# A late mask build, DMA transposes for half of a layernorm's blocks, and retuned instruction priorities in a fused attention and mixer layer

## The chip, the cores and the metric

The kernel runs on one core of one Trainium2 chip. The metric is the device time of the core in microseconds (us); a profile of one execution gives a span that is about 2 us shorter. A run counts as slow when it takes over 1.5% more than the fastest of its kernel. Engines: TensorE (PE; PEld is its weight load), VectorE (DVE), ScalarE (ACT), GpSimd (POOL), and SyncE (SP), which issues all DMAs of this kernel from one queue.

## The reference, cut to what matters

```
x [2048, 448] bf16
h   = x + A(layernorm(x))     # A: q,k,v = x@wqkv; 16 heads; each token sees 8 keys
                              #    at distances 0,2,..,14; softmax; @ wo
h2  = h + B(layernorm(h))     # B: z = gelu(x@w_in); z1, z2 = halves; z2 = layernorm(z2)
                              #    g = w_sp[2048,2048] @ z2 + b_sp; (z1*g) @ w_out
```

The token axis is cut into 16 blocks of 128. "LN1" is the first layernorm. QK products are made for groups of four blocks, so there are four QK groups of four TensorE pairs each. "Mixing" is the product with `w_sp`.

## The kernel before: the parts that matter

The program builds a graph of tasks. Each task has engines that may run it, an assumed duration, and a priority. A list scheduler then fixes the order of instructions on every engine when the kernel is built. Nothing is reordered on the chip: an engine runs its list in order and waits on semaphores. SP is such an engine too, and a DMA's assumed duration on it is the price of issuing it.

```
DMA_US = 2.6                                # assumed: from issue to landing
P = dict(ln_s=0.26, ln_o=5.43, qk_s=2.72, ..., npt=4, nlt=15)   # priorities, tuned by search

def dma_t(dst, src, us, ...):               # DMA transpose; callers pass us = 1.3
    return G.add([("sp", us)], [lambda e: e.dma_start(dst(), src(), transpose=True)], ...)

def layernorm(m, i, prio):                  # i = 0: LN1, i = 1: the second layernorm
    ... bn_stats, bn_aggr (DVE); rstd (POOL); normalise into tring[:, slot] (DVE)
    if i:                                   # second layernorm: one DMA transpose, 128x512
        dma_t(lambda: xB[:, m, :, :], lambda: tring[:, t.slot, :], 1.3, [t], [rm], prio)
        ...
        return
    # LN1: four 128x128 transposes on TensorE into PSUM, one copy out
    G.add([("pe", 0.27)], [e.transpose(psb[...], tring[:, t.slot, c*128:(c+1)*128], ident) for c in range(4)], ...)
    G.add([("act", ...), ("dve", ...)], [copy_on(e, xm, psb[...])], ...)     # xm = xT[:, :, 128m:128m+128]
    if m < P["npt"]:                        # swap of partition halves: two copies ...
        ... copy_on(e, um[ps, 0:3, :], xm[po, 0:3, :])
    elif m % 4 == 3:                        # ... or, for four blocks together, two DMAs
        dma(... e.dma_start(xU[dst, :, cols], xT[src, 0:3, cols]) ...)
```

A QK group needs `xT` (transposed LN1) and `xU` (the same with its partition halves swapped) of its four blocks. The ring `tring` has six slots.

The softmax here doesn't subtract the row's maximum and nothing guards it: scores larger than these inputs give would overflow.

## Time and profile before

The median is 261.2 us; the profiled span is 259.2 us.

| stage | us from the start |
|---|---|
| first statistics aggregated (DVE) | 6.80 |
| first QK pair starts | 16.9 |
| second QK group starts | 34.9 |
| third QK group starts | 47.8 |
| mixing starts | 138.2 |
| end | 259.2 |

From the page of the kernel before: busy tenths of TensorE in 40 equal slices of the span, and the TensorE clock granted, in tenths of full speed.

```profile
PE   6788699999999999799999999999999999999995
PEclk9999799999999999999999999999999999999999
```

TensorE is busy nearly everywhere after the fifth slice. In the fifth slice, the second of the two with a dip, the clock drops to 7 tenths, its lowest. The chain of waits (start us, duration us, what) of the kernel before:

```profile
4.39 1.32 DVE z1p L491
6.97 0.52 DVE st L557
...
16.98 6.17 PE psum L613 x56
...
29.70 1.50 PE psum L621 x4
...
34.95 6.15 PE psum L613 x56
...
106.02 3.23 DMA xS<-xB
...
138.20 10.74 PE psum L771 x49
```

L491 is an integer operation of the mask build. It stands behind the first block's statistics (2.88 us), but ahead of their aggregation (6.80 us) and of the statistics of the next blocks (L557). The four value matmuls at 29.70 us take 1.50 us, about twice the usual 0.77: the granted clock there was 0.50. TensorE had idled 3.0 us before, in three gaps of 0.5, 0.6 and 1.9 us. What SP issues between 20 and 60 us (timeline view; start, us, engine, line, operation, count):

```profile
24.77 1.29 SPq L594 DMA_DIRECT2D xU<-wsp  x2
26.11 4.00 SPq L529 DMA_DIRECT2D w<-in_B_w_in_dram  x6
43.18 2.63 SPq L594 DMA_DIRECT2D xU<-wsp  x4
51.69 5.00 SPq L450 DMA_TRANSPOSE xB<-tring  x3
```

And the second layernorm's DMA transposes, as the view of the tile `tring` gives them (duration in ns: min/median/max):

```profile
L450 SPq DMA_TRANSPOSE xB<-tring x16: 1188/1266/2611, 51.7 to 117.2; - x16
```

A 128x512 DMA transpose keeps the SP queue for about 1.27 us, and a half swap, a plain DMA, for about 0.62 us.

### The profile page before, as it was taken

To read this page: it belongs to the slowest core of one execution; us is meant where nothing else is said; L and a number is where in the kernel's file an instruction comes from. 1 tells how busy PE (TensorE), PEld (TensorE's weight loads), DVE (VectorE), ACT (ScalarE), POOL (GpSimd) and SP (SyncE) were. 2 spreads that over 40 slices of the span, in tenths; PEclk is the share of its full clock that TensorE was granted. 3 is DMA by queue.
4 is the path that set the end of the run, shared out by engine and by line. 5 is a ranking of instruction groups with operands and counts; after the bars stand their busy time and mean duration, and the time that the engine had idled before them with its cause. 6 is when DMAs were issued, how large, how long until landed. Compare 5 with 4: busy or idle time off the path is not lost.

```text
span 259.2 us, 5020 instructions
## 1 busy us (share of the span) xinstructions
PE 244.4 (94%) x2065; PEld 122.2 (47%) x2076; DVE 158.2 (61%) x359; ACT 97.0 (37%) x117; POOL 48.1 (19%) x123
## 2 busy tenths in 40 slices
PE   6788699999999999799999999999999999999995
PEld 2334455455556454355454444544444444444442
DVE  4989888977999999869880008433333333333333
ACT  2147768698897988456663000000000000000000
POOL 7444313220030335425350000000000000000000
PEclk9999799999999999999999999999999999999999
DMA  5992701332122545555436414444044440010002
GB/s 148 296 262 71 169 0 30 96 71 54 43 43 65 89 100 110 130 118 107 108 79 184 97 27 101 101 102 114 0 101 101 104 91 0 25 48 0 0 0 71
DMA packets 58102, 22.41 MB, mean 86 GB/s; under 512 B 48096, under 2 KB 56928, under 8 KB 58080
## 3 DMA queue, kind: packets, MB, share of 16 engines
q1 hardware_dynamic: 58080, 22.10, 36.4%
q8 instruction: 16, 0.26, 0.4%
q14 instruction: 6, 0.05, 0.1%
HBM read 6.49 MB, written 1.84 MB: 32 GB/s over the span
## 4 chain that ended last, share of the span: by engine, by line
PE 87%; DVE 5%; ACT 2%; POOL 1%; DMA 1%; issue 1%; SPq 1%; DVEq 0%; POOLq 0%
PE psum L771 37%; PE psum L613 25%; PE psum L621 10%; PE psum L789 8%; PE psum L675 3%; PE psum L654 2%; PE psum L687 2%; ACT z1p L663 1%; DMA xS<-xB 1%; DVE st L557 1%; PE psum L580 1%; SPq L450 1%; DVE xU L599 1%; DVE tring L562 1%; DVE z1p L491 1%
## 5 line engine op out<-in xcount | busy, mean ns | idle before, releaser
L776 DVE TENSOR_TENSOR qk<-psum,bb 128x512 bf16<-128x512 f32 x28 | 19.3, 690 | 68.3 <-PE psum L771 68.3
L771 PE MATMUL psum<-early,z2p 128*128 128x512 bf16 x218 | 48.5, 379 | 0.3
L771 PE MATMUL psum<-wsp,z2p 128*128 128x512 bf16 x219 | 48.4, 379 | 0.4 <-issue 0.2
L663 ACT ACTIVATE z1p<-psum 128x912 bf16<-128x912 f32 (+2 forms) x36 | 33.5, 933 | 3.4 <-PE psum L654 2.9
L771 PEld LDWEIGHTS psum<-wsp,z2p 128*128 128x128 bf16 x224 | 21.9, 98 | 26.5 <-issue 0.4
L771 PEld LDWEIGHTS psum<-early,z2p 128*128 128x128 bf16 x224 | 22.0, 98 | 26.3
L604 POOL TENSOR_TENSOR rstd<-va,mhalf 128x1 f32<-128x1 f32 x48 | 31.4, 656 | 3.8
L602 POOL TENSOR_SCALAR va<-mv 128x1 f32<-128x1 f32 x48 | 11.1, 233 | 81.4 <-DVE mv L559 64.4
L613 PE MATMUL psum<-wsp,early 64*128 64x512 bf16 x128 | 25.0, 376 | 0.0
L613 PE MATMUL psum<-w,xB 64*128 64x448 bf16 x112 | 22.8, 349 | 2.2 <-DMA xS<-xB 1.7
L613 PE MATMUL psum<-xU,early 64*128 64x512 bf16 x96 | 23.3, 377 | 0.0
L613 PE MATMUL psum<-w,xS 64*128 64x448 bf16 x112 | 22.9, 350 | 0.0
L598 ACT ACTIVATE qk<-psum 128x1024 bf16<-128x1024 f32 (+1 forms) x21 | 19.0, 909 | 7.8 <-PE psum L613 7.8
L789 PE MATMUL psum<-xS,z1p 128*128 128x448 bf16 x112 | 21.8, 352 | 0.0
L613 PE MATMUL psum<-xB,w 64*128 64x512 bf16 x98 | 21.8, 376 | 0.0
L613 PE MATMUL psum<-xS,w 64*128 64x512 bf16 x98 | 21.8, 376 | 0.0
L741 DVE BATCH_NORM_STATS2 st<-z2p 128x6 f32<-128x448 bf16 x32 | 19.4, 608 | 3.6 <-ACT z2p L737 3.1
L670 DVE TENSOR_TENSOR z1p<-z1p,maskb 128x1824 bf16<-128x1824 bf16 (+2 forms) x18 | 19.9, 1103 | 1.6 <-ACT z1p L663 1.5
L557 DVE BATCH_NORM_STATS2 st<-x_tm 128x6 f32<-128x448 bf16 x32 | 19.4, 605 | 1.6 <-DMA x_tm<-in_A_x_dram 1.5
L621 PE MATMUL psum<-early,wsp 128*128 128x448 bf16 (+2 forms) x72 | 17.4, 371 | 0.6 <-DVE wsp L599 0.5
L737 ACT ACTIVATE z2p<-psum 128x896 bf16<-128x896 f32 x16 | 14.4, 917 | 8.0 <-PE psum L613 8.0
L763 ACT ACTIVATE z1p<-psum 128x1024 bf16<-128x1024 f32 x14 | 14.3, 1023 | 8.2 <-PE psum L613 8.2
(67 smaller groups left out, 274.5 us busy)
## 6 DMA issues: line engine op xcount, KB each, us to landing
xS<-xB SPq DMA_DIRECT2D x16, 128.0 KB, 2.4
out_dram<-tring SPq DMA_DIRECT2D x16, 112.0 KB, 1.7
xU<-wsp SPq DMA_DIRECT2D x6, 192.0 KB, 3.0
x_tm<-in_A_x_dram SPq DMA_DIRECT2D x1, 896.0 KB, 8.7
w<-in_B_w_in_dram SPq DMA_DIRECT2D x8, 112.0 KB, 3.2
early<-in_A_wqkv_dram SPq DMA_DIRECT2D x2, 392.0 KB, 5.8
w<-in_B_w_in_dram SPq DMA_DIRECT2D x2, 392.0 KB, 7.9
xS<-in_B_w_out_dram SPq DMA_DIRECT2D x1, 784.0 KB, 4.5
```

Source lines behind the costliest of these rows:

```text
L557: G.add([("dve", dve_us(D))], [lambda e: e.bn_stats(st[:, s.slot, 0:6], x_tm[:, m, :])], [r_x[m]], [s], [s], prio=prio)
L598: return e.activation(dst, src, AF.Copy)
L604: G.add([("pool", 0.61)], [lambda e: e.tensor_tensor(rstd[:, k:k + 1], va[:, k:k + 1], mhalf[:, 0:1], ALU.pow)], [r_va[k], r_half], [r_rs[ ...
L613: return [lambda e, j=j, u=u: e.matmul(bank2(b, j, n), ws(j, (LO, HI)[j], u), xs(j, (LO, HI)[j], u), start=(u == 0), stop=(u == 6), tile_p ...
L621: return [lambda e, c=c: e.matmul(bank(b, n, 0, m), ws(ALL, c), xs(ALL, c), start=(c == 0), stop=(c == NCH - 1)) for c in range(NCH)]
L663: lambda e, hh=hh: e.activation(E[0:nk, ev.slot, hh * 4:hh * 4 + 8, 0:nq].rearrange("p (b g) q -> p b g q", b=2), banks(lb, hh, 512, nk).r ...
L670: lambda e: e.tensor_tensor(E[0:nk, ev.slot, :, 0:nq], E[0:nk, ev.slot, :, 0:nq], maskb[0:nk, mi:mi + 1, 0:nq].to_broadcast([nk, NHEAD, nq ...
L737: lambda e, zb=zb, m=m: e.activation(z2p[:, m, :].rearrange("p (b c) -> p b c", b=2), banks(zb, 0, D), AF.Gelu_apprx_tanh)],
L741: lambda e, h=h, m=m, s=s: e.bn_stats(st[:, s.slot, 6 * h:6 * h + 6], z2p[:, m, D * h:D * (h + 1)])],
L771: lambda e, s=s: e.matmul(bank(b, 512), z2p[:, s, fc * 128:(fc + 1) * 128], w[:, s, :], start=(s == 0), stop=(s == NB - 1)) for s in range ...
L776: G.add([("dve", dve_us(512))], [lambda e: e.tensor_tensor(ub[:, u.slot, :], bank(b, 512), bb[:, 512 * tc:512 * (tc + 1)], ALU.add)], [b, ...
L789: lambda e, f=f: e.matmul(bank(b, D), z1p[:, f, 128 * m:128 * m + 128], w_out[:, f, :], start=(f == 0), stop=(f == FC7 - 1)) for f in rang ...
```

## The change

The intent: take the mask build out of the way of the first layernorm; move LN1's transposes of blocks 8 to 15 from TensorE, and their copies from DVE and ScalarE, to the DMA queue; order the last output blocks; and choose the priorities anew for the new graph. Cut to its core:

```diff
+P_TR_US = 0.45
-P = dict(ln_s=0.26, ..., z0=74.82, ..., z1=110.69, ..., npt=4, nlt=15)
+P = dict(ln_s=0.9, ..., z0=150.45, ..., z1=116.86, ..., npt=8, nld=8, mc=25.81)
 ...   # the five mask operations
-            G.add([("dve", 0.2)], [fn], rd, wr, prio=-3.0)
+            G.add([("dve", 0.28)], [fn], rd, wr, prio=P["mc"])
 ...   # layernorm(m, 0, ...)
+            if m < P["nld"]:
                 (TensorE transposes and copy, as before)
+            else:
+                for c in range(NCH):
+                    G.add([("sp", P_TR_US)], [lambda e, c=c: e.dma_start(xm[:, c, :],
+                          tring[:, t.slot, 128 * c:128 * c + 128], transpose=True)],
+                          [t], [], adds=[rm], prio=prio)
 ...   # wout_block
-                    [b] if lo else [], prio=prio, keep=0 if lo else 1)
+                    [b] if lo else [], prio=prio + (m % 4) * 0.1 + (0.05 if lo else 0.0), keep=0 if lo else 1)
```

`npt=8` also moves the half swap of blocks 4 to 7 from DMAs to copies.

## The prediction

> **What bounds it now.** The busy table has TensorE at 94% of a 259.2 us span. By stretches (windows view), from 138 us to the end TensorE runs 28 mixing tiles and 16 output blocks with no gap (117.3 of 121 us); the change cannot shorten that. The time lost lies earlier.
> 1. Start. The chain of waits runs over POOL memsets, then the int32 mask operation (1.31 us on DVE at 4.39 us), then the first layernorm. DVE's statistics of block 0 begin at 2.88 us, but their aggregation runs only at 6.80 us, behind the mask build (2.5 us busy, 0.9 us wait). The first QK pair starts at 16.9 us.
> 2. After the first QK pairs, 24 to 29 us, TensorE idles some 3 us, and its granted clock falls to 0.50 from 30 to 32.5 us (four value matmuls take 1.50 us instead of 0.77). The second QK group starts only at 34.9 us. The Trainium skill ("TensorE: Matmul & The Clock Gate", rules for kernels) says idle of over about 3 us halves the clock; the trace agrees.
> 3. At 107.7 us TensorE waits 1.7 us for the swapped-half DMA of the last blocks.
> In 35 to 104 us TensorE, DVE (90%) and ScalarE (83%) are all nearly full.
>
> **What the change does.**
> - Mask build late: up to 2.5 us of DVE leaves the first layernorm's chain. The QK weights' DMA and their 7 copies (from 13.3 us) limit the gain: first QK pair at about 15 us, gain 1.5 to 2.5 us.
> - Blocks 8 to 15 by DMA: removes 32 transposes from TensorE (4 took 0.25 to 0.4 us) and 8 copies (DVE 0.42, ScalarE 0.60 us): about 2 us TensorE, 3.5 to 4.5 us DVE/ScalarE. Adds 32 DMA transposes on the SP queue. A 128x512 one takes 1.26 us to issue, 2.5 us to land; I estimate 0.3 to 0.6 us issue for a quarter. Latency per block grows from about 1 us to 3 or 4 us, then the half-swap DMA (3 us). SP is nearly idle at 15 to 50 us, so this should hide.
> - Half swap of blocks 4 to 7 by copies, not DMA: adds 8 copies of 0.29 us on DVE (or 0.48 on ScalarE), but lets QK group 2 start earlier and should fill part of loss 2 (gain 1 to 3 us).
> - Retuned priorities put the last z1 pairs ahead of z2, so loss 3 probably goes (1 to 1.7 us).
> - Ordered last blocks: the output blocks already run in this order by index; I expect nothing.
>
> **Sum.** 2 + 2 + 1.7 + 1.2 = about 7 us gross. DVE is nearly full and gains little net, and some of each gain returns as other waits; I keep 55 to 60%: about 4 us.
>
> Predicted 257.2 us, range 254.0 to 260.3. Faster by over 2%: 0.33; within 2%: 0.65; slower: 0.02.
>
> **What would show it.** First statistics aggregation near 4 us; first QK pair at 14.5 to 15.5 us; transposes on TensorE 32, not 64; half-clock stretch near 30 us shorter or gone; no wait for the swapped halves near 107 us; mixing begins at 133 to 135 us instead of 138.2; from there to the end still about 121 us.
>
> **What would make it wrong.** The DMA transposes issue slowly or land late, so QK groups 3 and 4 wait for them; the int32 mask operation falls into another critical place; DVE is the true limit and gives nothing back.

## The result, and the profile after

The change made the kernel slower: 284.15 us against 261.18 us, ratio 1.088 (95% interval 1.083 to 1.093). A ratio here and below is the mean time of one kernel's fast runs over that of the other's of the same rounds, so it is not quite the ratio of the medians quoted.

| stage | before | after |
|---|---|---|
| first statistics aggregated | 6.80 | 3.57 |
| first QK pair | 16.9 | 14.1 |
| second QK group | 34.9 | 28.2 |
| third QK group | 47.8 | 60.1 |
| mixing starts | 138.2 | 160.9 |
| end | 259.2 | 282.4 |

Up to the second QK group the change gained 6.7 us. At the third group it was 12.3 us behind. From the start of mixing to the end both need the same (121.0 and 121.5 us). The slices of the page after:

```profile
PE   6996993049449999998799999999999999999994
PEclk9998899559959999999999999999999999999999
```

The dips are in slices 7 to 9, 11 and 12 (between 42 and 85 us). The chain of waits there:

```profile
14.20 6.15 PE psum L619 x56
...
28.22 6.99 PE psum L619 x56
...
54.55 1.23 SPq L590
56.33 0.63 SPq L600
57.02 2.91 DMA xU<-wsp
60.06 6.62 PE psum L619 x42
...
76.03 1.27 SPq L451
77.86 0.60 SPq L600
78.50 3.10 DMA xU<-wsp
81.73 4.52 PE psum L619 x28
...
160.86 24.28 PE psum L777 x112
```

L590 is the new DMA transpose, L600 the half swap, L619 the QK pairs. The chain, which ran over TensorE before, now runs over the *issuing* of DMAs. The SP timeline says why:

```profile
27.00 5.94 SPq L590 DMA_TRANSPOSE wsp<-tring  x4
32.98 3.98 SPq L530 DMA_DIRECT2D w<-in_B_w_in_dram  x6
37.01 18.77 SPq L590 DMA_TRANSPOSE wsp<-tring  x14
56.33 1.30 SPq L600 DMA_DIRECT2D xU<-wsp  x2
57.67 18.31 SPq L590 DMA_TRANSPOSE wsp<-tring  x14
76.03 1.27 SPq L451 DMA_TRANSPOSE xB<-tring  x1
77.86 1.25 SPq L600 DMA_DIRECT2D xU<-wsp  x2
```

And the view of line L590, with TensorE's waits:

```profile
L590 SPq DMA_TRANSPOSE wsp<-tring x32: 1185/1232/2161, 27.0 to 74.8; - x32
```

```profile
PE psum L619 <- DMA xU<-wsp: 22.2, 2, 14.3
PE psum L619 <- DMA xS<-xB: 1.5, 1, 1.5
```

A 128x128 DMA transpose takes 1.23 us of SP, not the 0.45 us that the builder assumed, and not the quarter of the 128x512 price that I assumed. SP works through its list in order, so from 37.0 us the half swap stands behind 14 of them (18.8 us). TensorE waits 14.3 us before the third QK group and 7.9 us before the fourth: 22.2 us, against a loss in span of 23.2 us. SP had been idle before 27.0 us only because block 8 was not normalised yet; from there on it had no slack.

### The profile page after: what moved, and what is told of

It reads as the page before. It is cut to its first block, busy times and chain, and to the rows that moved or that the text cites. A ratio compares the mean times of both kernels' runs of the same rounds, so it can differ in the third digit from the quotient of the medians.

```text
span 282.4 us, 5019 instructions
## 1 busy us (share of the span) xinstructions
PE 246.5 (87%) x2044; PEld 121.1 (43%) x2044; DVE 155.7 (55%) x354; ACT 100.8 (36%) x122; POOL 49.9 (18%) x125
## 4 chain that ended last, share of the span: by engine, by line
PE 75%; DVE 8%; SPq 6%; DMA 3%; POOL 3%; ACT 2%; issue 2%; DVEq 0%; POOLq 0%
PE psum L777 34%; PE psum L619 22%; PE psum L795 7%; PE psum L627 7%; SPq L590 4%; DMA xU<-wsp 2%; PE psum L681 2%; SPq L451 2%; DVE z1p L676 2%; PE psum L660 1%; ACT z1p L669 1%; DVE st L747 1%; DVE tring L563 1%; DVE xU L605 1%; PE psum L693 1%
## 5 line engine op out<-in xcount | busy, mean ns | idle before, releaser
L619 PE MATMUL psum<-wsp,early 64*128 64x512 bf16 x128 | 29.3, 417 | 22.2 <-DMA xU<-wsp 22.2
L604 ACT ACTIVATE qk<-psum 128x1024 bf16<-128x1024 f32 (+1 forms) x26 | 21.8, 841 | 33.4 <-PE psum L619 33.4
L608 POOL TENSOR_SCALAR va<-mv 128x1 f32<-128x1 f32 x48 | 12.2, 254 | 95.6 <-DVE mv L560 77.2
L619 PE MATMUL psum<-xU,early 64*128 64x512 bf16 x96 | 27.1, 424 | 0.0
L619 PE MATMUL psum<-w,xB 64*128 64x448 bf16 x112 | 22.7, 350 | 2.8 <-DMA xS<-xB 1.5
L619 PEld LDWEIGHTS psum<-wsp,early 64*128 64x128 bf16 x128 | 11.3, 103 | 31.8 <-issue 25.2
L619 PE MATMUL psum<-w,xS 64*128 64x448 bf16 x112 | 22.7, 350 | 0.0
L619 PE MATMUL psum<-xB,w 64*128 64x512 bf16 x98 | 21.8, 377 | 0.0
L619 PE MATMUL psum<-xS,w 64*128 64x512 bf16 x98 | 21.8, 377 | 0.0
L747 DVE BATCH_NORM_STATS2 st<-z2p 128x6 f32<-128x448 bf16 x32 | 19.4, 606 | 3.6 <-ACT z2p L743 3.3
L558 DVE BATCH_NORM_STATS2 st<-x_tm 128x6 f32<-128x448 bf16 x32 | 19.4, 605 | 1.6 <-DMA x_tm<-in_A_x_dram 1.5
L769 ACT ACTIVATE z1p<-psum 128x1024 bf16<-128x1024 f32 x14 | 14.3, 1023 | 8.5 <-PE psum L619 8.5
L563 DVE TENSOR_SCALAR tring<-x_tm,mv,rstd 128x448 bf16<-128x448 bf16 x32 | 12.3, 392 | 9.1 <-DMA xB<-tring 6.6
```

The source lines that it names most:

```text
L558: G.add([("dve", dve_us(D))], [lambda e: e.bn_stats(st[:, s.slot, 0:6], x_tm[:, m, :])], [r_x[m]], [s], [s], prio=prio)
L563: G.add([("dve", 0.32)], [lambda e: e.tensor_scalar(tring[:, t.slot, 0:D], x_tm[:, m, :], mv[:, k, 0:1], rstd[:, k:k + 1], ALU.subtract, A ...
L604: return e.activation(dst, src, AF.Copy)
L619: return [lambda e, j=j, u=u: e.matmul(bank2(b, j, n), ws(j, (LO, HI)[j], u), xs(j, (LO, HI)[j], u), start=(u == 0), stop=(u == 6), tile_p ...
L747: lambda e, h=h, m=m, s=s: e.bn_stats(st[:, s.slot, 6 * h:6 * h + 6], z2p[:, m, D * h:D * (h + 1)])],
```

## Experiments

Theory A: each DMA transpose has a fixed issue price of about 1.23 us, whatever its size, and the in-order SP queue turns the sum of these prices into lateness of the half swap. Rivals: B, the transposing transfers themselves are slow (by bytes or by tiles); C, the retuned order is bad in itself; D, the issue price goes with the size of the DMA.

**The ordered last blocks need no run.** I applied that edit alone to the kernel before, and removed it alone from the changed kernel, and compared the built instruction lists. All five engines have the same lists with and without it. The blocks already ran in that order by their index. This part of the change does nothing.

### The number of DMAs per block: one, two, eight (the change has four)

In these three kernels the same elements go through the same path, and the price given to the scheduler for a whole block stays at 1.8 us. The lists of TensorE, DVE, ScalarE and POOL are identical to those of the changed kernel, the waits on semaphores apart; only SP's list differs.

```diff
-                for c in range(NCH):
-                    G.add([("sp", P_TR_US)], [... e.dma_start(xm[:, c, :], tring[:, t.slot, 128 * c:128 * c + 128], transpose=True)],
+                for c in range(0, NCH, 4):       # one_dma;  two_dma: step 2, c:c + 2, 256 columns, 2 * P_TR_US
+                    G.add([("sp", 4 * P_TR_US)], [... e.dma_start(xm[:, c:c + 4, :], tring[:, t.slot, 128 * c:128 * c + 512], transpose=True)],
```

```diff
+                for c, h in [(c, h) for c in range(NCH) for h in (0, 64)]:       # eight_dma
+                    G.add([("sp", P_TR_US / 2)], [... e.dma_start(xm[:, c, h:h + 64], tring[h:h + 64, t.slot, 128 * c:128 * c + 128], transpose=True)],
```

> The changed kernel with the four 128x128 DMA transposes of a block merged into one 128x512 DMA; the order of instructions on every engine but SP stays the same, and the same bytes go through the same transposing path. Theory A (each transposing DMA costs about 1.23 us of issue on the SP queue whatever its size; 32 of them delay the half-swap DMAs): SP issue of LN1 transposes falls from about 43 us to 8 x 1.25 = 10 us, the TensorE wait for the half-swap DMA falls from 22.2 us to under 2 us, time 258 to 260.5 us. Rival B (the transfers themselves are slow, by bytes or by tiles): no change, time 280 us or more, wait near 22 us. Rival C (the retuned order of TensorE is bad in itself): wait moves elsewhere, time stays over 270 us.

> The same with two 128x256 DMAs per block, 16 in all; order on the other engines unchanged. Theory A: from 37.0 us on the SP queue needs 7 x 1.25 us before the first half-swap instead of 14 x 1.25, so it is issued at about 46 us and lands near 50 us; TensorE waits about 4 us instead of 14.3, the second wait of 7.9 us nearly goes; time 261 to 265 us. Rival B: 280 us or more.

> The changed kernel with each block split finer: eight DMA transposes of 64x128 per block, 64 in all, the same bytes, order on the other engines unchanged. Theory A (a fixed issue cost of about 1.23 us for each transposing DMA): about 79 us of SP issue; before the first half-swap the queue needs 8 x 1.23 + 4 + 28 x 1.23 us from 27 us on, so it lands near 80 us instead of 60, the second near 118 us instead of 82; TensorE waits over 50 us, time about 320 us (310 to 330). Rival D (issue cost in proportion to the elements of the DMA, so 0.6 us each): no change, 282 to 286 us.

| DMAs per block (size) | median issue, us | sum of issue, us | wait for the half swap, us | time, us | ratio to before |
|---|---|---|---|---|---|
| 1 (128x512) | 1.29 | 10.3 | 0 | 259.7 | 0.992 (0.989 to 0.995) |
| 2 (128x256) | 1.25 | 20.0 | 4.1 | 263.2 | 1.004 (1.002 to 1.007) |
| 4 (128x128): the change | 1.23 | 39.4 | 22.2 | 284.2 | 1.088 (1.083 to 1.093) |
| 8 (64x128) | 1.23 | 78.6 | 62.5 | 326.5 | 1.248 (1.236 to 1.261) |

The sum of issue is count times median. The last row rests on two runs, the others on four. All three new times lie in the ranges that theory A gave. The views of L590 in one_dma, two_dma and eight_dma, one fence each:

```profile
L590 SPq DMA_TRANSPOSE wsp<-tring x8: 1190/1286/2285, 27.0 to 49.7; - x8
```

```profile
L590 SPq DMA_TRANSPOSE wsp<-tring x16: 1235/1247/2553, 27.0 to 55.0; - x16
```

```profile
L590 SPq DMA_TRANSPOSE wsp<-tring x64: 1089/1228/2435, 27.1 to 116.2; - x64
```

TensorE's waits in two_dma and in eight_dma; one_dma has no such line:

```profile
PE psum L619 <- DMA xU<-wsp: 4.1, 2, 2.8
```

```profile
PE psum L619 <- DMA xU<-wsp: 62.5, 2, 35.2
```

The price moves by no more than 0.06 us over a factor of eight in size, so D falls. Fewer DMAs for the same bytes take away 22 us of waiting, so B falls. Identical lists on the four other engines give anything from 260 to 326 us, so C falls as the cause of the slowdown. From four to eight DMAs per block, issue grows by 39.2 us and the time by 42.3 us; from two to four, by 19.4 and 21.0 us. From one to two, 9.7 us of issue cost only 3.5 us, because the queue still had slack. The SP timeline of one_dma shows that slack: the third group's swap is issued at 42.48 us and is no longer late.

```profile
33.28 9.03 SPq L590 DMA_TRANSPOSE wsp<-tring  x4
42.48 1.28 SPq L600 DMA_DIRECT2D xU<-wsp  x2
```

```profile
46.32 4.71 PE psum L619 x42
```

This is the third group in one_dma's chain of waits; the change has 60.06 us and 6.62 us there. eight_dma came out 6 us above the 320 us expected, inside the range given (310 to 330 us). Its mean clock was 0.89, against 0.96 in the changed kernel and 0.99 in one_dma.

The spans of the change and of one_dma differ by 24.4 us. The half-swap wait is 22.2 of it. After the two stalls the QK pairs run at a lowered clock: three pairs take 6.62 us against 4.71 in one_dma, and two pairs 4.52 against 3.20 in two_dma, together about 3.2 us. One_dma waits 1.8 us more for the second layernorm's swap (3.3 against 1.5 us). The sum, 22.2 + 3.2 - 1.8 = 23.6 us, leaves under 1 us unexplained.

### The late mask alone

```diff
-            G.add([("dve", 0.2)], [fn], rd, wr, prio=-3.0)     # in the kernel before
+            G.add([("dve", 0.28)], [fn], rd, wr, prio=25.81)
```

> The kernel before with only the mask build put late (its priority and its assumed cost as in the change). Both theories: first statistics aggregation near 3.6 us instead of 6.8, first QK pair 1 to 2.5 us earlier than 16.9 us; total 0.5 to 2 us faster than before, 259.2 to 260.7 us, because the loss at 24 to 35 us stays. If the mask build were a cause of the slowdown: slower than 262 us.

Measured: 260.43 us, ratio 0.993 (0.991 to 0.996), so 0.7% faster. Its chain of waits, at the two QK groups:

```profile
14.18 6.15 PE psum L613 x56
34.63 6.15 PE psum L613 x56
```

The first QK pair came 2.8 us earlier, more than expected, but the second group only 0.3 us earlier: most of the start's gain is not kept, as the other losses stay. The integer operation of the mask build also took only 0.19 us at its new place, 7.93 us, against 1.31 us before, where POOL was busy beside it; why was not isolated by a run. The scheduler moved some other instructions too (1999 of TensorE's 2076 keep their order, and SP's list is the same), so the 0.7% belongs to the new schedule as a whole. This part of the change is good and small.

### All transposes on TensorE, with the new priorities

```diff
-         npt=8, nld=8, mc=25.81)
+         npt=8, nld=16, mc=25.81)
```

> The changed kernel with all 16 blocks of LN1 transposed on TensorE as before (nld=16), priorities of the change kept though they were chosen for the DMA path. Theory A: no wait for half-swap DMAs over 1 us, SP queue free; the order is not tuned for it, so 264 to 269 us, i.e. slower than before but far below 284. Rival C (the new priorities and the copies for blocks 4 to 7 are to blame): 278 us or more.

Measured: 270.26 us, ratio 1.032 (1.027 to 1.036), 1.3 us above the expected range. There was no wait for LN1's half swap. But its order is not tuned, and it shows an order problem of its own. `w_out` is loaded into the memory of `xS`, so its DMA must wait until the last z1 pair (L619) has read `xS`. The kept priorities put that pair behind all of mixing, at 236.38 us. SP had nothing left to issue from 204 us on; the load went out as soon as the pair was done.

```profile
PE psum L795 <- DMA xS<-in_B_w_out_dram: 4.5, 1, 4.5
```

```profile
236.38 1.64 PE psum L619 x14
238.03 4.43 DMA xS<-in_B_w_out_dram
```

This wait is about half of the loss against the kernel before; the rest was not traced.

So the priorities of a searched schedule belong to the graph that they were searched for. This run is no fair comparison of the two ways to transpose. The next three are.

### Priorities searched again with measured prices

I gave the builder the measured prices and searched the priorities again, each time by many trials of the builder's own scheduling model (no chip). In all three kernels SP issue is priced at 0.62 us for a plain DMA; a DMA transpose of LN1 is one 128x512 DMA at 1.28 us. tuned_dma and tuned_pe also have landing 0.3 us later, ScalarE operations 0.04 to 0.08 us dearer, and the logits at 0.33 us instead of 0.22. Cut to its core:

```diff
-P_TR_US = 0.45 (four per block)
+one DMA per block, ("sp", 1.28)
-return G.add([("sp", 0.5)], [fn], ...)        # plain DMA
+return G.add([("sp", 0.62)], [fn], ...)
-DMA_US = 2.6
+DMA_US = 2.9                                   # tuned_dma, tuned_pe
-P = dict(ln_s=0.9, ln_o=-0.7, ..., npt=8, nld=8, mc=25.81)
+P = dict(ln_s=0.58, ln_o=2.51, qk_s=4.2, qk_o=-42.64, ..., npt=8, nld=10, mc=131.45)   # tuned_dma
+P = dict(ln_s=0.53, ln_o=-8.37, ..., npt=8, nld=8, mc=4.79)                            # tuned_dma8
+P = dict(ln_s=2.22, ln_o=-12.12, ..., npt=8, nld=16, mc=48.22)                         # tuned_pe
```

> One 128x512 DMA transpose per block, its price in the scheduling model set to the measured 1.28 us of SP issue, plain DMAs to 0.62 us and 0.3 us more to land, ScalarE operations 0.08 us dearer, and all priorities chosen anew for these prices (10 blocks of LN1 on TensorE, 6 by DMA). Theory A with the right price: no half-swap wait over 1 us, 255.5 to 259.5 us, faster than before and at least as fast as one_dma (259.7). If the DMA path were a loss in itself: slower than tuned_pe.

> The same, 8 blocks by DMA, with only the SP issue prices corrected (1.28 and 0.62 us) and the priorities chosen for them; the model then gives a span of 255.1 us. Its other prices are slightly optimistic, so 257 to 261 us; no long wait for half-swap DMAs.

> All 16 blocks of LN1 on TensorE, the same corrected prices and the same search of the priorities as tuned_dma: the fair counterpart of the DMA path, where pe_all (270.3 us) kept priorities made for another program. The model puts it 2.1 us behind tuned_dma. Expected 257.5 to 261.5 us, 0.5 to 3 us slower than tuned_dma. If it is 265 us or more, the other priorities of the change, not the missing DMA path, held pe_all back.

| kernel | LN1 blocks by DMA | time, us | ratio to before |
|---|---|---|---|
| tuned_dma | 6 | 258.23 | 0.987 (0.984 to 0.990) |
| tuned_dma8 | 8 | 258.20 | 0.991 (0.986 to 0.997) |
| tuned_pe | 0 | 259.67 | 0.995 (0.990 to 0.999) |

All three beat the kernel before (261.40 us in these rounds), if by less than 2%, and the change; all three times lie in the ranges expected. tuned_dma is the best version found by the mean of its runs (258.04 us, against 258.84 us for tuned_dma8; the medians are level): 1.3% faster than before and 26 us faster than the change. In its profile, the fastest of its four runs with a span of 255.1 us, the half-swap wait is down to:

```profile
PE psum L619 <- DMA xU<-wsp: 0.8, 1, 0.8
```

The DMA path is therefore no loss in itself: between tuned_dma and tuned_pe it is worth 1.4 us by the medians. But the two intervals meet at 0.990, and two searches are not equally lucky, so I would call the advantage likely and not settled.

### What could not be tried

Four DMAs per block with a price of 0.85 us or more could not be built with these priorities (0.8 us builds, but was not run): the list scheduler ran out of tasks that it could start. The same happened to one_dma with the mask build put back early at its old price of 0.2 us (at 0.28 us it builds, but was not run), and with `npt=4`, so the half-swap copies of blocks 4 to 7 were not isolated. A ring of eight `tring` slots did not fit into SBUF.

## Why the prediction was wrong, point by point

- **The step that failed** is the price in "Adds 32 DMA transposes on the SP queue ... I estimate 0.3 to 0.6 us issue for a quarter." It measured 1.23 us. I had one size in the trace, 128x512 at 1.27 us, and divided by four. One point cannot say whether a price goes with the size. The same step went on to "SP is nearly idle at 15 to 50 us, so this should hide". With the right price the sum was 32 x 1.23 = 39.4 us, to be issued after 27.0 us, when the first normalised block was ready. TensorE stood ready for the third group at 45.7 us, 18.7 us later. The 16 transposes of its four blocks alone need 16 x 1.23 = 19.7 us of SP, and the half swap has to be issued and to land (0.6 and 2.9 us) after them. It could not hide. That turned a forecast gain of 4 us into a loss of 23 us.
- I listed "the DMA transposes issue slowly or land late, so QK groups 3 and 4 wait for them" among what would make it wrong. That is what happened, but I gave "slower" a chance of 0.02 only. A risk that can be named and priced from the trace should have been priced. The Trainium skill ("VectorE: DVE Perf Modes", the three transpose paths) gives 1309 ns for a DMA transpose of 128x128. The 1.23 us of issue here is close to it, and so even the estimate for a quarter had a better source than my division.
- **Late mask**: right, and undersized. First aggregation at 3.57 us ("near 4"), first QK pair at 14.1 us against the forecast 14.5 to 15.5, a gain of 2.8 us for 1.5 to 2.5. Alone it gives the whole kernel 0.7%.
- **Half swap of blocks 4 to 7 by copies**: the second QK group did start earlier, by 6.7 us. How much of that is due to the copies and how much to the new priorities was not isolated. In one_dma, where no transposing DMA is late, the third group starts at 46.3 us, only 1.5 us before the 47.8 us of the kernel before: the head start is not kept.
- **Clock**: forecast as "shorter or gone" near 30 us; it moved. From 25 to 30 us the granted clock after was 0.66, and from 22 to 35 us its mean was 0.87 in the kernel before and in one_dma. Two new drops, to 0.50, came with the stalls.
- **Wait near 107 us**: forecast gone; the change has a 1.5 us wait for `xS` and 1.0 us of issue, one_dma 3.3 us for `xS` against 1.7 before. The new order of z1 and z2 did not remove it.
- **Ordered last blocks**: right, nothing; shown by the identical lists. **From mixing to the end**: "about 121 us", measured 121.5. **Start of mixing** at 133 to 135 us: wrong, 160.9 us, for the reason above.
- With one DMA per block in place of four and nothing else (one_dma, 259.7 us) the kernel falls into the range predicted (254.0 to 260.3), 2.5 us above its middle. That does not show the rest of the sum to be right: in the same rounds one_dma gained 0.8% and late_mask alone 0.7%, with intervals that overlap. So beyond the late mask no gain of the DMA path, the copies or the new order is shown clear of the noise, where the sum had counted about 5 of its 7 us gross.

## What to carry to other kernels

Here a DMA transpose was paid per instruction on the queue that issued it (1.23 to 1.29 us from 64x128 to 128x512): merge the pieces of a block into one DMA before moving transposes there, and count issue time per queue as you count busy time per engine, from the moment that its first input is ready to the moment that its output is due. When an order is fixed by a scheduler with assumed prices, a wrong price on one in-order engine gives an order that waits, and the other engines' lists need not change at all to cure it. Before a price is scaled to another size, look for two sizes in a trace, or measure the price by changing only the number of pieces.

## What the Trainium skill lacked or had wrong

- "DMA: Bandwidth & Descriptors", DMA Transpose (X-bar): it gives constraints, but no issue cost named for this chip. A table elsewhere on the page has a column of cycles for "previous generations", which names no chip. Here a DMA transpose out of SBUF takes 1.23 to 1.29 us of the SP queue for 64x128, 128x128, 128x256 and 128x512 alike, so in this range the cost is per DMA and not per element. A plain DMA took about 0.61 us (the half swap of 192 KB).
- The same page, Issuing engines are not separate DMA queues, says of the time to initiate a DMA that it "is usually small relative to the DMA itself". In the changed kernel issue was 1.23 us against a landing of 2.4 us after it, and the sum of issue, 39.4 us, was what delayed the kernel, while the DMA engines' mean busy share from 35 to 104 us was 0.27.
- "VectorE: DVE Perf Modes", the three transpose paths: the 1309 ns for 128x128 bf16 by DMA does not say whether it is issue, transfer or latency. Here issue alone is 1.23 us and landing follows about 2.4 us after it; and 128x512 costs the same issue, so per 128x128 piece the cost can be a quarter of the entry.
- "Advanced Engine Details and Errata", X-Bar Transpose (TRN2), says that transpose DMAs are as fast as regular ones. In issue they were not: 1.23 us against 0.61 us.
- "TensorE: Matmul & The Clock Gate", Why this matters for your kernels, asks for no idle gap of over about 3 us between bursts of matmuls, as the clock else falls back to half. The long stalls agree: in the waits of 14.3 and 7.9 us the granted clock fell to 0.50, and QK pairs ran slower after them (6.62 us for three instead of 4.71). But the length of one gap did not decide alone. In the kernel before, the clock fell to 0.50 at 30 us after gaps of 0.5, 0.6 and 1.9 us, and in two_dma it stayed at 1.00 through a gap of 2.8 us. Why is not shown.
